# One decode step on one core: the last of wo's 32 row groups loaded on all 128 partitions, not on 64

## The chip, the core and the metric

The kernel runs on one core of a Trainium2 chip. The metric is device time in microseconds of one launch. The median of three runs of the kernel before is 100.18 us; the runs lie between 100.13 and 102.2 us. The profiled execution took 100.13 us, of which its page covers a span of 98.7 us, from the first instruction to the last.

## What is computed

One token `x` (1 x 1024, bf16) goes through an attention layer and an MLP that stand side by side, and the results are added.

```python
def reference(x, k_cache, v_cache, wq, wo, w1, b1, w2, b2):
    xn = layernorm(x)
    # attention: 32 query heads, 4 key/value heads of 128, the last 4096 positions
    q = xn @ wq                               # wq 1024 x 4096
    p = softmax(q k^T / sqrt(128));  o = p v  # per head
    attn = o.reshape(4096) @ wo               # wo 4096 x 1024
    # MLP on the layernorm of xn
    h = gelu(layernorm(xn) @ w1 + b1)         # w1 1024 x 3584
    mlp = h @ w2 + b2                         # w2 3584 x 1024
    return x + attn + mlp
```

With one token every weight is used once, so the kernel is a stream of loads with small products behind it: wq 8 MB, keys 4 MB, w1 7 MB, values 4 MB, w2 7 MB, wo 8 MB (counted as 1024 x 1024 bytes). The matmuls have the token's numbers as the stationary operand (128 x 1) and 512 columns of the weight as the moving one.

## The kernel before

All large loads are issued by the SyncE queue, in the order in which they are used: the first part of wq, the keys, the rest of wq, w1 in two halves, the values. w2 goes into the buffer of w1, and wo into the buffer of wq, so these loads wait until the second half of the w1 product is done (`pe_h`). The part that the change touches begins there.

`wo_pm` lays the 4096 rows of wo out so that partition p holds rows 32p to 32p+31; below, "row group r" is row 32p+r for every p, 2 KB on each of 128 partitions, 256 KB in all. Groups 0 to 30 are loaded into `WA` in seven pieces of 12, 9, 4, 2, 2, 1 and 1 groups. Group 31 is loaded apart, in eight small loads into the old key buffer `KT`: it is laid on partitions 0 to 63 alone, two rows (`s`) beside each other on each partition, and each small load covers eight partitions that lie four apart.

```python
WO_CHUNKS = [12, 9, 4, 2, 2, 1, 1]
...
wo_pm = A_wo.rearrange("(p j) n -> p (j n)", j=32)
wo_e = A_wo.rearrange("(s q e c j) n -> j q c e s n", s=2, q=2, e=8, c=4, j=32)
...
sp.wait_ge(PE.sem, pe_h)
c0 = 0
for j, nch in enumerate(W2_CHUNKS):                       # w2: 14 and 14
    sp.dma_start(W2[:, ...], w2_pm[:, ...]).then_inc(s_w2[j], 16)
    ...
j0 = 0
for j, nj in enumerate(WO_CHUNKS):
    sp.dma_start(WA[:, j0 * D:(j0 + nj) * D], wo_pm[:, j0 * D:(j0 + nj) * D]).then_inc(s_wo[j], 16)
    j0 += nj
    if j == 0:
        for q in range(2):
            for c in range(4):
                p0 = 32 * q + c
                sp.dma_start(KT[p0:p0 + 29:4, 0:2 * D].rearrange("e (s n) -> e s n", s=2),
                             wo_e[31, q, c]).then_inc(s_we, 16)
```

The attention output is put on 128 partitions as `OP`, one column for each row group. Because group 31 lies on 64 partitions, the upper half of the last column is copied down to partitions 0 to 63 as well (`OPX`).

```python
dve.wait_ge(PE.sem, pe_op)
DVE.mark(dve.tensor_copy(OP[:, :], PS[:, 512: 512 + 32]))
d_op = DVE.mark(dve.tensor_copy(OPX[:, :], PS[64:128, 512 + 31: 512 + 32]))
pe.wait_ge(DVE.sem, d_GT)
for j in range(len(W2_CHUNKS)):
    w2_rows(j)                                            # 56 matmuls into ACC[0], ACC[1]
```

The product with wo comes last. TensorE waits for each piece of wo, and multiplies two halves of 512 columns for each row group into the same accumulators as w2. After the first piece it does group 31 in four matmuls of 64 partitions. The output row is then copied out of PSUM, half by VectorE and half by ScalarE, and stored.

```python
pe.wait_ge(DVE.sem, d_op)
r = 0
for j, nj in enumerate(WO_CHUNKS):
    pe.wait_ge(s_wo[j], 16)
    for _ in range(nj):
        for n in range(2):
            last = pe.matmul(ACC[n], lhsT=OP[:, r:r + 1], rhs=WA[:, ...],
                             start=False, stop=(r == 30))
        r += 1
    if j == 0:
        pe.wait_ge(s_we, 8 * 16)
        for lhsT, c in ((OP[0:64, 31:32], 0), (OPX[:, :], D)):
            for n in range(2):
                pe.matmul(ACC[n], lhsT=lhsT, rhs=KT[0:64, c + n * 512: c + (n + 1) * 512],
                          start=False, stop=False)
pe_fin = PE.mark(last)
dve.wait_ge(PE.sem, pe_fin)
d_out = DVE.mark(dve.tensor_copy(OUT[32:33, :], ACC[1]))
act.wait_ge(PE.sem, pe_fin)
a_out = ACT.mark(act.activation(out=OUT[0:1, :], in_=ACC[0], func=ACTF.Copy))
```

Of the kernel before, what the change touches and what calls it, by code (L numbers as in the profile page):

```python
# [4 lines left out]
dt = mybir.dt  # L5
# [4 lines left out]
D = 1024  # L10
# [11 lines left out]
WQ_CHUNKS = [1, 3, 4]  # L22
W1_CHUNKS = [4, 4]
W2_CHUNKS = [14, 14]
WO_CHUNKS = [12, 9, 4, 2, 2, 1, 1]


class Track:
# [11 lines left out]
def bass_parallel_sum__sliding_block_cached__mixer_channel_mlp__decode_kernel(  # L40
# [20 lines left out]
    pe, dve, act, pool, sp = nc.tensor, nc.vector, nc.scalar, nc.gpsimd, nc.sync  # L61
# [7 lines left out]
    s_v = [nc.alloc_semaphore(f"s_v{g}") for g in range(HKV)]  # L69
    s_w2 = [nc.alloc_semaphore(f"s_w2{j}") for j in range(len(W2_CHUNKS))]  # L70
    s_wo = [nc.alloc_semaphore(f"s_wo{j}") for j in range(len(WO_CHUNKS))]
    s_we = nc.alloc_semaphore("s_we")
    s_out = [nc.alloc_semaphore(f"s_out{n}") for n in range(2)]

    PE = Track(nc, "S_PE")
    DVE = Track(nc, "S_DVE")
# [3 lines left out]
    def sb(name, shape, dtype):  # L80
        return nc.alloc_sbuf_tensor(name, shape, dtype)
# [37 lines left out]
    OHF = sb("OHF", [32, DH], dt.float32)  # L119
    OH = sb("OH", [32, DH], dt.bfloat16)  # L120
    OP = sb("OP", [128, 32], dt.bfloat16)
    OPX = sb("OPX", [64, 1], dt.bfloat16)
    OUT = sb("OUT", [33, 512], dt.bfloat16)
    KV = sb("KV", [128, HKV * W + HKV * NBLK * DH], dt.bfloat16)
    KT = KV[:, 0:HKV * W]
# [4 lines left out]
    PS = nc.alloc_psum_tensor("PS", [128, 8 * 512], dt.float32)  # L130

    ACC = [PS[32 * n: 32 * n + 1, (6 + n) * 512: (7 + n) * 512] for n in range(2)]
# [5 lines left out]
    w1_pm = B_w1.rearrange("(p k) n -> p (k n)", k=KC)  # L138
    w2_pm = B_w2.rearrange("(p c) n -> p (c n)", c=FC)
    wo_pm = A_wo.rearrange("(p j) n -> p (j n)", j=32)  # L140
    wo_e = A_wo.rearrange("(s q e c j) n -> j q c e s n", s=2, q=2, e=8, c=4, j=32)
    out_row = out.rearrange("b s n -> (b s) n")


# [14 lines left out]
    r = 0  # L159
# [136 lines left out]
    for j, nr in enumerate(WQ_CHUNKS):  # L296
        pe.wait_ge(s_wq[j], 16)
        for _ in range(nr):
            for n in range(2):
                for t in range(4):  # L300
                    c = k * NQ + t * 1024 + n * 512
                    last = pe.matmul(  # L302
                        PS[32 * t: 32 * t + 1, n * 512:(n + 1) * 512],
                        lhsT=XNTb[:, k:k + 1], rhs=WA[:, c: c + 512],
                        start=(k == 0), stop=(k == KC - 1))
# [19 lines left out]
    for i in range(4):  # L325
        p0, p1 = 32 * i, 32 * (i + 1)
# [11 lines left out]
    for g in range(HKV):  # L338
        for j in range(4):
            u = g * 4 + j  # L340
            for n in range(2):
                rhs = KT[:, g * W + n * 2048: g * W + (n + 1) * 2048].rearrange(
                    "p (b j a) -> p b j a", j=4, a=32)[:, :, j, :]
                last = pe.matmul(  # L344
                    PS[:, (4 + n) * 512:(5 + n) * 512],
                    lhsT=LQ[:, u * 128:(u + 1) * 128], rhs=rhs,
                    start=(u == 0), stop=(u == 15))
# [6 lines left out]
    for n in range(2):  # L354
        for t in range(4):
            pe.matmul(PS[32 * t: 32 * t + 1, (2 + n) * 512:(2 + n) * 512 + HW],  # L356
                      lhsT=identb[0:8, 2 * t + n: 2 * t + n + 1], rhs=B1R[:, :],
                      start=True, stop=False)
# [54 lines left out]
    j0 = 0  # L413
    for j, nj in enumerate(WO_CHUNKS):
        sp.dma_start(WA[:, j0 * D:(j0 + nj) * D], wo_pm[:, j0 * D:(j0 + nj) * D]).then_inc(s_wo[j], 16)  # L415
        j0 += nj
        if j == 0:

            for q in range(2):
                for c in range(4):  # L420
                    p0 = 32 * q + c
                    sp.dma_start(KT[p0:p0 + 29:4, 0:2 * D].rearrange("e (s n) -> e s n", s=2),  # L422
                                 wo_e[31, q, c]).then_inc(s_we, 16)


    dve.wait_ge(PE.sem, pe_h)
# [26 lines left out]
    for r in range(4):  # L453
        n = r // 2
        pe.matmul(ACC[n][:, (r % 2) * 256:(r % 2 + 1) * 256],
                  lhsT=identb[:, 32 * r: 32 * r + 1], rhs=XR[:, :],
                  start=False, stop=False)
# [16 lines left out]
    for b in range(NBLK):  # L474
        last = pe.matmul(PS[0:32, 0:512].rearrange("p (g d) -> p g d", g=HKV),  # L475
                         lhsT=PT[:, b * 32:(b + 1) * 32], rhs=Vb[:, b, :, :],
                         start=(b == 0), stop=(b == NBLK - 1))
# [25 lines left out]
    for q in range(4):  # L503
        last = pe.matmul(PS[:, 512: 512 + 32],
                         lhsT=SEL[:, q * 128:(q + 1) * 128], rhs=OH[:, q * 32:(q + 1) * 32],
                         start=(q == 0), stop=(q == 3))
    pe_op = PE.mark(last)
    dve.wait_ge(PE.sem, pe_op)
    DVE.mark(dve.tensor_copy(OP[:, :], PS[:, 512: 512 + 32]))
    d_op = DVE.mark(dve.tensor_copy(OPX[:, :], PS[64:128, 512 + 31: 512 + 32]))  # L510
    pe.wait_ge(DVE.sem, d_GT)
    for j in range(len(W2_CHUNKS)):
        w2_rows(j)
# [3 lines left out]
# [5 lines that stand above are left out]
                last = pe.matmul(  # L522
                    ACC[n], lhsT=OP[:, r:r + 1],
                    rhs=WA[:, r * D + n * 512: r * D + (n + 1) * 512],
                    start=False, stop=(r == 30))
            r += 1
        if j == 0:
            pe.wait_ge(s_we, 8 * 16)
            for lhsT, c in ((OP[0:64, 31:32], 0), (OPX[:, :], D)):
                for n in range(2):  # L530
                    pe.matmul(ACC[n], lhsT=lhsT, rhs=KT[0:64, c + n * 512: c + (n + 1) * 512],
                              start=False, stop=False)
    pe_fin = PE.mark(last)

    dve.wait_ge(PE.sem, pe_fin)
# [39 lines left out]
```

## Time and profile before

| | |
|---|---|
| median of three runs | 100.18 us |
| span of the profile | 98.7 us |
| TensorE busy with matmuls | 51.5 us (52% of the span), 342 matmuls |
| VectorE busy | 35.8 us (36%) |
| ScalarE, GpSimd busy | 5.8 us, 4.6 us |
| moved by DMA | 39.89 MB, mean 404 GB/s over the span |
| mean granted TensorE clock | 0.844 |

On the page, "L415" is line 415 of the kernel, "SPq" is the queue of SyncE that issues the loads, and PE is TensorE. A row such as `PE PS L522` stands for matmuls at line 522 that write the PSUM tensor `PS`. "DMA WA<-in_A_wo_dram" in the chain means that the next step waited for a load of wo into `WA`. The row of digits called "DMA" gives, for each of 40 equal slices, the mean busy share of the core's 16 DMA engines in tenths. Beside the page, the trace holds one record for each packet of a DMA engine (start, duration, bytes, queue), and one for each increment by which a load reports to its semaphore: a load over 128 partitions leaves 16 of these, which come one by one as the DMA engines finish their shares. The prediction calls them the completion records.

### The profile page before, as it was taken

To read this page: it belongs to the slowest core of one execution; us is meant where nothing else is said; L and a number is where in the kernel's file an instruction comes from. 1 tells how busy PE (TensorE), PEld (TensorE's weight loads), DVE (VectorE), ACT (ScalarE), POOL (GpSimd) and SP (SyncE) were. 2 spreads that over 40 slices of the span, in tenths; PEclk is the share of its full clock that TensorE was granted. 3 is DMA by queue.
4 is the path that set the end of the run, shared out by engine and by line. 5 is a ranking of instruction groups with operands and counts; after the bars stand their busy time and mean duration, and the time that the engine had idled before them with its cause. 6 is when DMAs were issued, how large, how long until landed. Compare 5 with 4: busy or idle time off the path is not lost.

```text
span 98.7 us, 834 instructions
## 1 busy us (share of the span) xinstructions
PE 51.5 (52%) x342; PEld 17.8 (18%) x342; DVE 35.8 (36%) x54; ACT 5.8 (6%) x11; POOL 4.6 (5%) x15
## 2 busy tenths in 40 slices
PE   0002600009100945999974006999469950799961
PEld 0002200002000302344331002334123310222210
DVE  4338599999991053000449700000440000000002
ACT  0500150000000002000040000000000000000002
POOL 6830000000000000000000000000000000000000
PEclk9999999999975588599999855559975998557999
DMA  5999999989999989999999999999998999999950
GB/s 153 425 426 425 425 455 458 468 382 438 425 425 467 465 384 407 500 390 407 389 422 422 428 525 398 395 500 395 402 465 384 468 428 393 411 421 398 404 198 1
DMA packets 3394, 39.89 MB, mean 404 GB/s; under 512 B 432, under 2 KB 448, under 8 KB 1088
## 3 DMA queue, kind: packets, MB, share of 16 engines
q1 hardware_dynamic: 3362, 39.85, 95.6%
q8 instruction: 2, 0.03, 0.1%
q10 hardware_dynamic: 30, 0.01, 0.0%
HBM read 39.86 MB, written 0.00 MB: 404 GB/s over the span
## 4 chain that ended last, share of the span: by engine, by line
DMA 53%; SPq 23%; PE 18%; DVE 3%; issue 1%
DMA WA<-in_A_wq_dram 29%; DMA WA<-in_A_wo_dram 24%; SPq L415 14%; PE PS L344 9%; SPq L422 6%; PE PS L302 4%; PE PS L368 3%; SPq L153 2%; DVE TT L311 1%; SPq L411 1%; DVE OUT L536 1%; DVE LQ L331 1%; SPq L149 1%; PE PS L356 0%; PE PS L522 0%
## 5 line engine op out<-in xcount | busy, mean ns | idle before, releaser
L291 DVE STREAM_TRANSPOSE KV<-KV 128x4096 bf16<-128x4096 bf16 x4 | 17.4, 4413 | 0.0
L302 PE MATMUL PS<-WA,XNTb 128*1 128x512 bf16 x64 | 7.3, 621 | 17.2 <-DMA WA<-in_A_wq_dram 17.2
L475 PE MATMUL PS<-KV,PT 128*32 128x512 bf16 x32 | 10.0, 489 | 6.2 <-DMA KV<-in_A_v_cache_dram 6.2
L522 PE MATMUL PS<-WA,OP 128*1 128x512 bf16 x62 | 10.3, 474 | 5.4 <-DMA WA<-in_A_wo_dram 5.4
L536 DVE CAST OUT<-PS 1x512 bf16<-1x512 f32 x1 | 0.7, 683 | 23.8 <-PE PS L522 23.8
L344 PE MATMUL PS<-KV,LQ 128*128 128x512 bf16 x32 | 8.8, 443 | 0.7 <-DVE LQ L331 0.7
L495 PE MATMUL PS<-W,GT 128*1 128x512 bf16 x56 | 7.9, 452 | 0.0
L475 PEld LDWEIGHTS PS<-KV,PT 128*32 128x32 bf16 x32 | 3.7, 118 | 12.0 <-issue 10.1
L302 PEld LDWEIGHTS PS<-WA,XNTb 128*1 128x1 bf16 x64 | 1.7, 109 | 22.0 <-DMA WA<-in_A_wq_dram 19.1
L480 DVE TENSOR_TENSOR OHM<-PS,RM 32x512 f32<-32x512 f32 x1 | 0.7, 680 | 13.3 <-PE PS L475 13.3
L522 PEld LDWEIGHTS PS<-WA,OP 128*1 128x1 bf16 x62 | 2.8, 96 | 12.8 <-issue 7.6
L256 PE MATMUL PS<-XT,onesf 128*128 128x16 f32 x2 | 0.6, 383 | 7.6 <-DVE XT L252 7.6
L344 PEld LDWEIGHTS PS<-KV,LQ 128*128 128x128 bf16 x32 | 3.5, 111 | 5.6 <-issue 2.3
L377 DVE TENSOR_REDUCE MXP<-PS 128x1 f32<-128x1024 f32 x1 | 1.2, 1224 | 8.9 <-PE PS L344 8.9
L495 PEld LDWEIGHTS PS<-W,GT 128*1 128x1 bf16 x56 | 2.7, 96 | 4.8 <-issue 2.3
L368 PE MATMUL PS<-W,YTb 128*1 128x448 bf16 x64 | 3.4, 352 | 0.0
L311 DVE STREAM_TRANSPOSE TT<-PS 128x1024 f32<-128x1024 f32 x1 | 1.2, 1250 | 5.6 <-PE PS L302 5.6
L538 ACT ACTIVATE OUT<-PS 1x512 bf16<-1x512 f32 x1 | 0.6, 586 | 40.9 <-PE PS L522 40.9
L398 ACT ACTIVATE Pe<-PS,NMB 128x512 bf16<-128x512 f32 x2 | 1.3, 683 | 12.4 <-DVE NMB L395 12.4
L333 ACT ACTIVATE LQ<-PS 32x128 bf16<-32x128 f32 x2 | 0.5, 268 | 24.0 <-PE PS L318 23.9
L186 DVE MEMSET PS<- 128x2048 f32 x1 | 1.8, 1765 | 0.4 <-issue 0.4
L218 POOL MEMSET LQ<- 128x2176 bf16 x1 | 1.9, 1902 | 0.0
(87 smaller groups left out, 27.5 us busy)
## 6 DMA issues: line engine op xcount, KB each, us to landing
W<-in_B_w_dram SPq DMA_DIRECT2D x4, 3584.0 KB, 30.6
KV<-in_A_k_cache_dram SPq DMA_DIRECT2D x4, 1024.0 KB, 9.8
WA<-in_A_wq_dram SPq DMA_DIRECT2D x1, 4096.0 KB, 28.5
KV<-in_A_v_cache_dram SPq DMA_DIRECT2D x4, 1024.0 KB, 50.4
WA<-in_A_wq_dram SPq DMA_DIRECT2D x1, 3072.0 KB, 19.4
WA<-in_A_wo_dram SPq DMA_DIRECT2D x1, 3072.0 KB, 31.6
WA<-in_A_wo_dram SPq DMA_DIRECT2D x1, 2304.0 KB, 30.7
WA<-in_A_wq_dram SPq DMA_DIRECT2D x1, 1024.0 KB, 5.1
```

What stands on the lines that cost most here:

```text
L153: sp.dma_start(KT[:, g * W:(g + 1) * W], A_k_cache[0, g, SK - W:SK, :].rearrange("(m b) d -> m (b d)", m=128),).then_inc(s_k[g], 16)
L218: c_lq = POOL.mark(pool.memset(LQ[:, :], 0.0))
L291: d_k.append(DVE.mark(dve.transpose(out=KT[:, g * W:(g + 1) * W], in_=KT[:, g * W:(g + 1) * W])))
L302: last = pe.matmul(PS[32 * t: 32 * t + 1, n * 512:(n + 1) * 512], lhsT=XNTb[:, k:k + 1], rhs=WA[:, c: c + 512], start=(k == 0), stop=(k == ...
L311: DVE.mark(dve.transpose(out=TT[:, :], in_=PS[:, 0:1024]))
L344: last = pe.matmul(PS[:, (4 + n) * 512:(5 + n) * 512], lhsT=LQ[:, u * 128:(u + 1) * 128], rhs=rhs, start=(u == 0), stop=(u == 15))
L368: last = pe.matmul(PS[32 * t: 32 * t + 1, (2 + n) * 512:(2 + n) * 512 + HW], lhsT=YTb[:, k:k + 1], rhs=W1[:, c: c + HW], start=False, stop ...
L415: sp.dma_start(WA[:, j0 * D:(j0 + nj) * D], wo_pm[:, j0 * D:(j0 + nj) * D]).then_inc(s_wo[j], 16)
L422: sp.dma_start(KT[p0:p0 + 29:4, 0:2 * D].rearrange("e (s n) -> e s n", s=2), wo_e[31, q, c]).then_inc(s_we, 16)
L475: last = pe.matmul(PS[0:32, 0:512].rearrange("p (g d) -> p g d", g=HKV), lhsT=PT[:, b * 32:(b + 1) * 32], rhs=Vb[:, b, :, :], start=(b == ...
L495: pe.matmul(ACC[n], lhsT=GT[:, c:c + 1], rhs=W2[:, c * D + n * 512: c * D + (n + 1) * 512], start=False, stop=False)
L522: last = pe.matmul(ACC[n], lhsT=OP[:, r:r + 1], rhs=WA[:, r * D + n * 512: r * D + (n + 1) * 512], start=False, stop=(r == 30))
```

## The change

Row group 31 is loaded like the others: it becomes part of the first piece of wo, which grows from 12 to 13 row groups, on all 128 partitions. The eight small loads, the semaphore they report to, the copy `OPX` and the four matmuls on 64 partitions are gone, and two matmuls on 128 partitions are added for the 32nd row group. It is meant to keep every row group in one layout and to give the 16 DMA engines equal shares of it. The order of scores and the first half of h, which the title of the change also names, is the same in both kernels.

```diff
-WO_CHUNKS = [12, 9, 4, 2, 2, 1, 1]
+WO_CHUNKS = [13, 9, 4, 2, 2, 1, 1]
...
-    s_we = nc.alloc_semaphore("s_we")
...
-    OPX = sb("OPX", [64, 1], dt.bfloat16)
...
-    wo_e = A_wo.rearrange("(s q e c j) n -> j q c e s n", s=2, q=2, e=8, c=4, j=32)
...
         sp.dma_start(WA[:, j0 * D:(j0 + nj) * D], wo_pm[:, j0 * D:(j0 + nj) * D]).then_inc(s_wo[j], 16)
         j0 += nj
-        if j == 0:
-
-            for q in range(2):
-                for c in range(4):
-                    p0 = 32 * q + c
-                    sp.dma_start(KT[p0:p0 + 29:4, 0:2 * D].rearrange("e (s n) -> e s n", s=2),
-                                 wo_e[31, q, c]).then_inc(s_we, 16)
...
-    DVE.mark(dve.tensor_copy(OP[:, :], PS[:, 512: 512 + 32]))
-    d_op = DVE.mark(dve.tensor_copy(OPX[:, :], PS[64:128, 512 + 31: 512 + 32]))
+    d_op = DVE.mark(dve.tensor_copy(OP[:, :], PS[:, 512: 512 + 32]))
...
-                    start=False, stop=(r == 30))
+                    start=False, stop=(r == 31))
             r += 1
-        if j == 0:
-            pe.wait_ge(s_we, 8 * 16)
-            for lhsT, c in ((OP[0:64, 31:32], 0), (OPX[:, :], D)):
-                for n in range(2):
-                    pe.matmul(ACC[n], lhsT=lhsT, rhs=KT[0:64, c + n * 512: c + (n + 1) * 512],
-                              start=False, stop=False)
```

## The prediction

> **What bounds the kernel now.** I read the chain of waits first, from its end:
>
> ```profile
> 72.63 23.65 DMA WA<-in_A_wo_dram
> 96.28 0.04 issue
> 96.33 0.40 PE PS L522 x2
> 96.73 0.02 issue
> 96.75 0.68 DVE OUT L536
> ```
>
> The columns are start, length and what was waited for. The last load of wo lands at 96.28 us; behind it stand two matmuls, the copy of the output and its store, a fixed tail of about 2.4 us up to 98.7. So the end is the landing of the last piece plus a constant. The waits say the same of TensorE, and the page of the load stream:
>
> ```profile
> PE PS L522 <- DMA WA<-in_A_wo_dram: 5.4, 4, 4.2
> ```
>
> ```profile
> DMA  5999999989999989999999999999998999999950
> ...
> q1 hardware_dynamic: 3362, 39.85, 95.6%
> q8 instruction: 2, 0.03, 0.1%
> ```
>
> The 16 DMA engines are busy almost from the first slice to the last but one, so the question is what the change does to the work of the engine that finishes last. The "q8" line is the one to notice: two packets of instructions went over the same engines, though not in the load queue. The last 6 us of the DMA view (window 91 to 97) show that the engines do not finish together:
>
> ```profile
> DMA  9798999999999999999987676676452000000000
> GB/s 464 328 492 328 355 382 382 437 410 437 423 410 396 369 437 382 396 410 396 382 328 287 232 287 246 246 273 259 191 191 96 27 0 0 0 0 0 0 0 0
> ```
>
> A slice is 0.15 us. The rate falls from about 400 to about 250 GB/s at some 94.2 us and stays there for over a microsecond. A group of engines is idle by then while others work. The completion records name the groups. For three pieces of wo, the 16 times in order (us):
>
> ```
> groups 0-11  : 82.50 82.63 82.63 82.70 82.72 82.75 82.80 82.81 82.81 82.85 82.89 82.93 83.04 83.27 | 84.35 84.46
> groups 12-20 : 88.12 88.13 88.20 88.30 88.34 88.77 | 89.36 89.59 89.61 89.64 89.67 89.72 89.77 89.85 | 89.87 89.97
> group 30     : 94.52 94.52 94.59 94.69 94.74 95.11 | 95.69 95.89 95.93 95.94 95.97 96.03 96.08 96.13 | 96.16 96.28
> ```
>
> Before the small loads of group 31 there are 14 engines together and two **late** ones, 1.1 to 2.0 us behind. After them there are six early engines and ten late ones. Eight of the ten must be those that the small loads went to: the 8 loads left 72 completion records, 8 of them at 54.59 to 59.61, one soon after each issue, and 64 at 82.71 to 84.68, which is 8 engines for each load. The other two are the two that were late already. They cannot be among the eight, or they would be late twice, near 91.4 instead of 89.97. So the load of group 31 sits on eight engines that don't hold the two late ones, and it makes them just as late.
>
> Where do the two come from? The record of w1's first half (39.74 to 40.50) has no straggler; its second half has one (15 by 49.01, the last at 50.08); w2's first half still one (67.46, then 68.54); its second half two (75.95, then 77.05 and 77.16). The two instruction packets are at 42.77 us (16384 bytes, 1.069 us) and 69.83 us (16384 bytes, 1.061 us). Each falls between a record without and a record with one more straggler, and its length is the gap. In the DMA view of window 42 to 44 and of window 69 to 71 there is one such packet each:
>
> ```profile
> q1 hardware_dynamic: 30, 0.86, 101.6%
> q8 instruction: 1, 0.02, 3.3%
> ```
>
> [...] in a stream that is full, the packet pushes back one engine's later loads by 1.07 us, and nothing gives that back.
>
> **The change part by part.**
>
> *Removed: the eight small loads.* On each of the eight engines they are 8 x 2 packets of 2 KB. The trace has these 128 packets at a mean of 84 ns, so 16 x 0.084 = 1.34 us, and eight completion writes of 9 ns, 0.07 us: 1.4 us. The records agree: the medians of the early six and of the middle eight of groups 12-20 are 88.25 and 89.66.
>
> *Added: 2 KB on each of 128 partitions in the first piece.* That is 8 packets on each of 16 engines that grow from 24 to 26 KB. The mean packet of 24576 bytes takes 914 ns, that of 28672 bytes 1069 ns, so 2048 bytes more cost 155 / 2 = 78 ns, and eight of them 0.62 us. As a check, one more row group on its own moves the last record from 95.66 (group 29) to 96.28 (group 30), 0.62 us.
>
> *Sum at the last piece of wo, by group of engines:*
>
> | engines | last record now | change | then |
> |---|---|---|---|
> | the eight with small loads | 96.13 | -1.4 + 0.62 | 95.35 |
> | the six early | 95.11 | +0.62 | 95.7 |
> | the two behind an instruction packet | 96.28 | +0.62 | 96.9 |
>
> Total work falls a little (8 x 0.78 saved against 8 x 0.62 added), but only the last row counts: **+0.62 us**. I don't take off anything for the two engines having the memory to themselves at the end: 2 KB packets that start after 95.4 us, when few run, still take 84 ns.
>
> *SyncE.* The eight issues take 5.83 us of its queue (53.36 to 59.19), and wo's other pieces will be issued that much sooner. That is worth nothing: the last three issues already stall (4.48, 7.41 and 7.26 us) with loads queued ahead of them, and the last is issued at 79.89, some 15 us before its data come.
>
> *TensorE.* Four matmuls of 64 partitions go and two of 128 come. The first piece starts at 84.60 and gets 24 matmuls done by 89.8 at a granted clock of about half (0.53 in 84.5 to 90.4), 0.43 us a pair; group 31 follows until 90.43. Afterwards the start is near 85.2, and 13 pairs take 5.6 us, until 90.8. The second piece lands at 89.97 + 0.62 = 90.6, so there is 0.2 us of backlog, which goes by at the full clock that holds from 90.4 (1.00 in the table by stretches): nine pairs in 1.9 us, and the next piece lands at 93.1. The last pieces wait for data, as now.
>
> *VectorE.* The copy `OPX` (0.16 us at 72.83) lies 11 us ahead of its use. Nothing.
>
> Sum: 98.7 + 0.6 = 99.3 us of span, 100.18 + 0.62 = **100.8 us**.
>
> **The rivals.** (1) *The bytes are spread evenly, so the end comes sooner.* Over sixteen equal engines, removing 1.4 us from eight and adding 0.62 to all would bring the end 0.8 us forward, to 99.4. For it speaks that the middle eight end only 0.15 us before the last. Against it: the two late engines get the added bytes and none of the relief. It holds only if the stragglers change engine, or if the instruction packets fall elsewhere. Both packets come ahead of the first changed TensorE instruction, so I see no cause for that. (2) *TensorE becomes the end.* If the clock stayed at half for the rest, 32 pairs from 85.2 would last 13.7 us, to 98.9, about 2 us later than the data: near 102.8. The clock was at full from 90.4 and the load on TensorE hardly changes, so this is only a tail; it is why the range reaches further upward. (3) *Hidden anyway.* If the last piece of wo had slack, the time would not move. The chain shows none: 0.04 us between the landing and the matmul.
>
> **The range and the chances.** The step is 0.62 us if the late engines are the same two. Packet lengths could make it 0.4 to 0.9. The runs before spread upward (100.13, 100.18, 102.2), so I take 100.3 to 101.5. Two per cent are 2.0 us: slower by over that needs rival 2 (0.02), faster by over that nothing here would give (0.01).
>
> **What would show it.** The "KV<-in_A_wo_dram" issues are gone and the first piece of wo is 3328 KB. The last landing in the chain is near 96.9 instead of 96.28, the tail after it the same. The two instruction packets are again near 42.8 and 69.8. The completion records of the last piece fall into 14 together by about 95.7, and two near 96.8 and 96.9. If all 16 come together at about 95.5, the stragglers were not what I took them for; if the chain ends in a run of matmuls without a wait for data, it is rival 2.

## The result: 0.4 us slower, as the late engines would have it

The changed kernel takes 100.59 us (median of five runs, 100.44 to 100.9) against 100.18 us, a ratio of 1.0044 (95% interval 1.0022 to 1.0065). That is slower by 0.2 to 0.65%, well inside 2%, and 0.2 us under the predicted 100.8. It holds against the lower of two groups of times that the kernel before turned out to have; over all runs taken side by side later, the means of the two kernels lie 0.07 us apart (last experiment below). The ratios here and below leave out runs more than 1.5% above the fastest of the same kernel; what is left of the kernel before can still mix its two groups.

The chain of waits of the changed kernel, from its end (start, length, what was waited for), has the same form as before and has moved as a whole:

```profile
56.88 39.83 DMA WA<-in_A_wo_dram
96.70 0.04 issue
96.75 0.40 PE PS L511 x2
97.15 0.02 issue
97.17 0.68 DVE OUT L519
```

The last piece of wo lands at 96.70 us instead of 96.28; the two matmuls, the copy and the gaps have the lengths of before. The load starts much earlier in this chain (issued at 56.88, not 72.63), as the small loads no longer stand in SyncE's queue, and lands later all the same.

The page shows the stream as full as before, and again two packets of instructions:

```profile
DMA  5999999989999989989799998998998989999930
...
q1 hardware_dynamic: 3170, 39.85, 95.1%
q8 instruction: 2, 0.03, 0.1%
```

The DMA view of the last 6 us (window 91 to 97, slices of 0.15 us) has changed its form:

```profile
DMA  9999899999999997999999997421111111100000
GB/s 410 437 437 410 328 492 382 437 382 437 410 410 437 382 437 301 382 396 396 396 382 396 396 369 273 150 82 55 55 41 55 55 41 55 41 0 0 0 0 0
```

Before, ten engines shared the last microsecond at about 250 GB/s. Now the full rate holds until 94.6 us, nearly all engines stop together, and for a further microsecond some 55 GB/s are left. The completion records show two engines behind it, so about 27 GB/s each. For the piece with groups 0-12 and for the last one:

```
groups 0-12 : 83.26 83.27 83.31 83.32 83.33 83.34 83.38 83.39 83.44 83.47 83.51 83.55 83.57 83.66 | 84.89 84.90
last piece  : 95.15 95.16 95.19 95.21 95.22 95.23 95.26 95.28 95.31 95.36 95.38 95.42 95.45 95.53 | 96.69 96.70
```

Fourteen engines are done by 95.53, two by 96.70. (The last piece now holds the 32nd group.) The instruction packets were at 42.78 and 75.98 us.

### The profile page after: what moved, and what is told of

It is laid out like the page before. It is cut to its first block, busy times and chain, and to the rows that moved or that the text cites. A ratio compares the mean times of both kernels' runs of the same rounds, so it can differ in the third digit from the quotient of the medians.

```text
span 99.1 us, 821 instructions
## 1 busy us (share of the span) xinstructions
PE 51.1 (52%) x340; PEld 17.7 (18%) x340; DVE 35.6 (36%) x53; ACT 5.8 (6%) x11; POOL 4.6 (5%) x15
## 4 chain that ended last, share of the span: by engine, by line
DMA 69%; PE 19%; SPq 6%; DVE 3%; issue 1%
DMA WA<-in_A_wo_dram 40%; DMA WA<-in_A_wq_dram 29%; PE PS L341 10%; PE PS L299 4%; PE PS L365 3%; SPq L412 3%; SPq L150 2%; DVE TT L308 1%; SPq L408 1%; DVE OUT L519 1%; DVE LQ L328 1%; SPq L146 0%; PE PS L353 0%; PE PS L511 0%; PE PS L389 0%
## 5 line engine op out<-in xcount | busy, mean ns | idle before, releaser
L511 PE MATMUL PS<-WA,OP 128*1 128x512 bf16 x64 | 9.7, 441 | 7.2 <-DMA WA<-in_A_wo_dram 7.1
L465 PE MATMUL PS<-KV,PT 128*32 128x512 bf16 x32 | 9.3, 462 | 4.9 <-DMA KV<-in_A_v_cache_dram 4.9
L341 PE MATMUL PS<-KV,LQ 128*128 128x512 bf16 x32 | 10.0, 489 | 0.7 <-DVE LQ L328 0.7
```

Of the source, the lines that this page charges most:

```text
L341: last = pe.matmul(PS[:, (4 + n) * 512:(5 + n) * 512], lhsT=LQ[:, u * 128:(u + 1) * 128], rhs=rhs, start=(u == 0), stop=(u == 15))
L511: last = pe.matmul(ACC[n], lhsT=OP[:, r:r + 1], rhs=WA[:, r * D + n * 512: r * D + (n + 1) * 512], start=False, stop=(r == 31))
```

## The experiments

The theory: two DMA engines are late because each carried one packet of TensorE's instructions, and the two alone set the end; so what counts is what those two are given. Main rival: the two engines are late for another reason.

### Taking the instruction packets away

```diff
 # in short: the changed kernel; 61 of 340 matmuls stay, all waits and loads as they were
-for u in ...: for n in range(2): matmul(scores)      +only u == 0
-for b in range(NBLK): matmul(p v)                    +only b == 0
-for c in w2 chunk / r in wo piece / k in w1 half     +only the first of each; q: row 0 and two matmuls
```

> The changed kernel with most matmuls left out (57 of 340 stay, so TensorE has about 115 matmul and weight-load instructions, fewer than the 170 it had begun when the first instruction packet came). All loads and their order stay; the output is not the reference's. Theory (two DMA engines are late because each carried one packet of TensorE's instructions): no instruction packet beside the loads, the 16 completion records of the last piece of wo within 0.5 us of each other, near 95.5 instead of 96.70, a span near 98.0 and a time near 99.4, about 1.1 us less than the changed kernel and 0.8 below the kernel before. Rival (the two engines are slower for a reason of their own, or for the load stream's sake): two records stay about 1.2 us behind and the last landing stays near 96.7.

It leaves out most of the arithmetic (61 matmuls stay, not the 57 of the forecast), so its time is that of the stream of loads with little behind it. Measured: 99.5 us (ratio to the kernel before 0.9885, 0.9805 to 0.9966), 1.1 us under the changed kernel. The queues on its page hold no instruction packet any more:

```profile
q1 hardware_dynamic: 3170, 39.85, 96.0%
q10 hardware_dynamic: 30, 0.01, 0.0%
```

Its DMA view of window 91 to 97 has no tail, and its chain starts the end at 95.45:

```profile
DMA  9999989999999999999999995200000000000000
```

```profile
54.09 41.36 DMA WA<-in_A_wo_dram
95.45 0.04 issue
```

All 16 records of the last piece lie between 95.07 and 95.45. The same loads in the same order, without the packets: no late engine. The rival that the engines are slow in themselves, or for the sake of the loads, falls. That it is the packets, and not the matmuls that went with them, rests on the next experiment as well.

### One packet more

```diff
+        for _ in range((80, 48, 0)[j]):     # while TensorE waits for wq
+            pe.matmul(PS[64:65, 3328:3336], lhsT=XNTb[:, 0:1], rhs=XNTb[:, 0:8], start=True, stop=True)
```

> The changed kernel with 128 tiny matmuls more (256 TensorE instructions), in the two gaps in which TensorE waits for wq. Their result is not used. Theory: one more packet of 16384 bytes of instructions, so three records of the last piece of wo behind the others, or one of them twice as far (about 2.2 us); in the first case the end moves by less than 0.3 us, in the second it is near 97.8, a time near 101.7. Rival (engines slow in themselves): two late records as in the changed kernel, whatever TensorE fetches.

The page and the chain:

```profile
q8 instruction: 3, 0.05, 0.2%
```

```profile
56.66 39.98 DMA WA<-in_A_wo_dram
96.64 0.04 issue
```

The third packet is at 16.6 us, and the records of the last piece end 95.41 | 96.51 96.60 96.64: three late engines in place of two, each late once. The time is 100.55 us (median of 20 runs), that of the changed kernel. So each packet of 16384 bytes makes one engine late (the 256 added instructions brought one), and the end here doesn't care how many are late, only how late the last is.

How late is more than the gap of 1.1 us to the record before, which belongs to the slowest of the other engines. Against the median of the others the three are 1.3 to 1.5 us behind, and the two of the changed kernel 1.4. The packet records of these two profiles show two parts: an instruction packet takes 0.98 to 1.11 us, and within 0.02 us of its end there starts a load packet that takes 1.46 to 1.57 us, 0.5 us more than the mean of its size (in the changed kernel 1.57 us against 1.07 for 28 KB, and 1.46 against 0.99 for 26 KB). The packet and this extra time together are about 1.5 us. (The records don't name the engine; that it is the same one is inferred from the times.)

### The old layout without the packets

The kernel before, with the same matmuls left out (65 of 342 stay, not 59).

> The kernel before with the same matmuls left out as in the changed kernel with few matmuls (59 stay; the output is not the reference's), loads and their order unchanged. Theory: no instruction packet, so the last landing is that of the eight engines with the small loads, near 96.1, against 95.45 in the changed kernel without packets: with the late engines gone, spreading group 31 evenly is now the better choice by about 0.65 us, and this kernel is at 100.0 to 100.2 us, no faster than with its packets. For the spread of the kernel before (a group near 100.1 to 100.5, a group near 101.4 to 101.9): if that comes from instruction packets on engines that also carry the small loads, this kernel has one group only, within 0.4 us. Rival (the spread comes from the small loads alone): a second group about 1.3 us higher stays.

Measured: 100.25 us (ratio 0.9988, 0.9968 to 1.0008). The tail of ten engines has become one of eight; DMA view of window 91 to 97, and the end of the chain:

```profile
DMA  6979989999999999999975545555532000000000
```

```profile
96.22 0.04 issue
96.26 0.61 PE PS L523 x2
```

The records of the last piece are eight at 94.53 to 94.78 and eight at 95.87 to 96.22. Against 95.45 with even shares, the small loads on eight engines now cost 0.77 us at the last landing (0.65 was expected), and the times of the two kernels without packets, 100.25 and 99.5 us, differ by 0.75. **This is the whole change in one table**, last landing of wo in one profile each:

| | with instruction packets | without |
|---|---|---|
| small loads on eight engines (before) | 96.28 | 96.22 |
| even shares (changed) | 96.70 | 95.45 |

The small loads on eight engines cost nothing only if late engines stand among the other eight, since the eight then finish just ahead of them. Even shares win 0.8 us in the stream without late engines, and lose 0.4 in the one with two.

### Which engines are late

```diff
+for m in range(1, 16):      # behind the last piece of wo: 64 bytes on each of m partitions
+    sp.dma_start(KT[0:m, ...32 elements...], wo_pm[0:m, 0:32]).then_inc(s_pr[m - 1], 16)
```

No record names its engine, so engines are numbered here by probe, from 0: engine 11 is the one that a probe of 12 partitions adds to those of a probe of 11. A first form had probes of 2 KB on 9 to 15 partitions behind the first piece of wo:

> The changed kernel with seven probe loads behind the first piece of wo, of 9, 10, 11, 12, 13, 14 and 15 partitions, 2 KB each, into the old key buffer; nothing reads them. [...] Theory (the two late engines are fixed ones outside the first eight): the loads of few partitions show no late record, and from some number on one and then two records are late by about 1.2 us; the numbers at which they appear name the two engines. Rival (the late engines are among the first eight and the small loads of the kernel before went elsewhere): both late already in the load of 9. The end is some 0.5 us later than in the changed kernel at most, 96.8 to 97.2.

The probe of 11 partitions has no late record (the last at 85.33), that of 12 has one (86.61, the others by 85.52), that of 13 two (86.60 and 86.79). So engines 11 and 12 are late. That each partition of a probe has an engine of its own, and that a larger probe uses the engines of the smaller ones and one more, was the author's assumption; one late record from 12 partitions on and two from 13 fit it. But the run took 102.42 us with the last landing at 98.61, over a microsecond later than expected: probes of this size disturb what they look at. So the probes were made tiny and put behind everything, in both kernels.

> The kernel before with fifteen tiny probe loads (64 bytes on each of 1, 2, ... 15 partitions[...]) behind the last piece of wo. A late engine shows in every probe from its number on, so the probes name the two engines behind the instruction packets. New theory, from the spread of the kernel before in the runs so far (a group near 100.1, a group near 101.3): the instruction packets do not keep to fixed engines, but go to neighbouring engines, others in each execution. If both named engines are among numbers 8 to 15: last landing of wo near 96.3, time near 100.2. If one is among 0 to 7, which also carry the small loads of group 31: last landing 97.3 to 97.7, time near 101.3. Rival (the packets always go to the same engines, 11 and 12 as in the probed run so far): those two again, and near 100.2.

> The changed kernel with the same fifteen probes behind the last piece of wo. New theory: two neighbouring late engines, whichever they are, last landing 96.5 to 96.9 and a time of 100.4 to 100.9, the same for all engine numbers, as all engines have equal shares. Rival (fixed engines): 11 and 12.

> The kernel before with the fifteen probes once more. New theory: other engine numbers than in the first run of it; with both among 8 to 15 the time is near 100.2 and the last landing near 96.3, with one among 0 to 7 near 101.3 and 97.3 to 97.7. Rival (fixed engines): the same numbers and the same time as in the first run.

The fifteen probes, of 120 partitions in all, bring 240 packets of under 512 bytes to the kernel before (672 in the first of these runs against 432), which fits one of data and one that reports for each partition. The data records of four probes of the first of these runs. The small loads of group 31 keep engines 0 to 7 busy up to 96 us and later: the probes of eight or fewer partitions have no data record before 96 us, the one of nine has its first at 94.94.

```
11 partitions: 95.03 95.09 95.27             | 96.84 96.98 97.08 97.23 97.50 97.58 97.84 98.30
12 partitions: 95.20 95.26 95.44 96.30       | 97.05 97.17 97.28 97.42 97.67 97.75 98.01 98.48
13 partitions: 95.38 95.43 95.63 96.34 96.48 | 97.26 97.38 97.48 97.61 97.86 97.93 98.19 98.66
14 partitions: 94.98 95.56 95.61 95.80 96.52 96.67 | 97.47 ...
```

Engines 8 to 10 are early (95.03 to 95.27 in the probe of 11 partitions), 11 and 12 are late (96.34 and 96.48 in that of 13), 13 is early again: the probe of 14 has four early records and two late ones. The second run of it says the same (with 12 partitions a record at 96.73 is new, with 13 one at 96.27), and so does the changed kernel (new records at 96.98 and 96.79, then at 95.46 with 14). The times are 101.01 and 100.52 us for the kernel before and 100.63 us for the changed one, with the wait for the probes at the end of each; the last landings of wo are 96.31, 96.56 and 96.80. So in every profiled execution that was probed the late engines are 11 and 12, outside the first eight. The theory that they change from one execution to the next found no support here; it falls for these executions.

### Even shares, but in eight small loads

```diff
-WO_CHUNKS = [13, 9, 4, 2, 2, 1, 1]
+WO_CHUNKS = [12, 9, 4, 2, 2, 1, 1]
+for i in range(8):          # behind the first piece
+    sp.dma_start(WA[16*i:16*(i+1), 31*D:32*D], wo_pm[16*i:16*(i+1), 31*D:32*D]).then_inc(s_we, 16)
...                         # TensorE waits for s_we and does group 31 behind the first piece
```

> Group 31 apart as in the kernel before, in eight small loads behind a first piece of 12 groups, but each of 16 partitions into its place on all 128 partitions: as many small loads and as much time of SyncE's queue as before, with every engine getting 16 KB as in the changed kernel. Theory (only which engines get the bytes matters): the last landing near that of the changed kernel, 96.7 to 96.9, two records behind 14; time 100.5 to 100.8. Rival (the small loads or their issue are what makes the kernel before faster): as the kernel before, 100.2, last landing 96.3.

A miss. The last landing is at 97.96, the time 101.76 us (1.0111, 1.0052 to 1.017). (The eight issues took 3.7 us of SyncE's queue, not the 5.8 of the kernel before; the longest stall behind them is 7.4 us in both. The page has 496 packets of under 512 bytes against 368 of the changed kernel, so 16 reports for each small load; the kernel before has 432, so eight.) So it is not the number of small loads that helped the kernel before. But equal shares alone don't make it the changed kernel either: the 128 packets of 2 KB took a mean of 117 ns (84 in the kernel before), and the 128 packets of 18 KB of the next piece up to 1285 ns, with a mean of 776 against 692. Together that is 128 x 33 ns + 128 x 84 ns = 15 us of engine time, 0.9 us on each of 16, most of the 1.1 to 1.3 us by which the last landing is later than in the changed kernel (96.70 and 96.83). A guess was that engines hinder each other when they write to neighbouring partitions, so the same loads were laid eight partitions apart.

> The eight small loads of 16 partitions again, each on partitions eight apart instead of 16 neighbours. Theory (16 engines that write to neighbouring partitions hinder each other): the packets of 2 KB take a mean of 84 to 100 ns instead of 117, the last landing comes down from 97.96 to 96.7 to 97.4, and the time to between 100.6 and 101.2. Rival (eight small loads on 16 engines cost this much wherever they are laid): 97.8 to 98.0, time near 101.8.

The guess falls: a mean of 122 ns, last landing at 98.26, 101.84 us (1.0101, 1.0071 to 1.0132). The chains of the two runs:

```profile
66.64 31.32 DMA WA<-in_A_wo_dram
97.96 0.04 issue
```

```profile
66.82 31.44 DMA WA<-in_A_wo_dram
98.26 0.04 issue
```

What does slow them stays open. The small loads of the kernel before lie four partitions apart, go to eight engines and write to `KT` (84 ns a packet); these go to 16 engines and write to `WA`, on neighbouring partitions (117 ns) or eight apart (122 ns). Spacing, engines and buffer changed together, and no run here parts them.

### The kernels again, and the spread of the kernel before

> The changed kernel itself, beside many runs of the kernel before. New theory: its runs lie close together, 100.4 to 100.9, between the two groups of the kernel before (near 100.1 and near 101.3), so that the means of both kernels differ by less than 0.3 us when both groups of the kernel before turn up. Theory of the prediction as it stands (the late engines never carry the small loads): all runs of the kernel before near 100.2, the changed kernel 0.4 to 0.6 us slower.

> The kernel before as it is, a look for an execution of its slower group. If its time is over 101: records of the last piece of wo with one or two engines 2.2 to 2.8 us behind the first (small loads and an instruction packet on the same engine), last landing near 97.5. If the slower group has another cause: 14 engines and two as in the known execution, and the time lost elsewhere. If it is near 100.2: last landing near 96.3 again.

> The same kernel again, with the same two readings: near 100.2 with the last landing near 96.3, or over 101 with one or two engines 2.2 to 2.8 us behind the first.

The changed kernel: 100.65 us over 22 runs (100.47 to 100.94), ratio 1.0031 (1.0012 to 1.005), last landing 96.83. The kernel before, profiled twice more: 100.18 us both times, last landings 96.21 and 96.33. Neither was an execution of the higher group, so that group was never seen in a profile.

There is such a group: of 97 runs of the kernel before beside these experiments, 57 lie between 99.79 and 100.53 us and 40 between 101.01 and 101.95. The changed kernel shows none of it in its 22 runs here, and the kernel before without instruction packets has 21 of 22 runs between 100.05 and 100.49, the other at 102.65. Counting all runs beside it, the changed kernel has a mean of 100.67 and the kernel before one of 100.60 (27 runs). So the forecast of two groups with equal means came true, and the theory that all runs of the kernel before lie near 100.2 did not.

An instruction packet on an engine that also carries the small loads would make such a group, and only in that kernel. Its size fits: an engine that ends near 96.1 and is put back by 1.5 us would end near 97.6, an estimated 1.3 us after 96.28, and the medians of the groups (100.2 and 101.42) are 1.2 us apart. But it is argued from the two absences, and not shown: no profile of that kernel has an engine that late. The experiment without packets also takes away most of TensorE's work. The granted clock does not tell the groups apart: it lies between 0.844 and 0.931 in the lower and between 0.846 and 0.932 in the higher.

## Why the prediction was right

**The end is a landing plus a constant.** Right: 2.42 us from the last landing to the end of the span before (96.28 to 98.7), 2.4 after (96.70 to 99.1).

**Two engines are late by an instruction packet each.** Right, and shown by taking the packets away and adding one. Two details were not. The cost of a packet is not its own length of 1.07 us: that is the gap to the slowest other engine, and in groups 0-11 of the kernel before the two late records are 1.5 and 1.7 us behind the median of the other fourteen. The sum was not touched by this, as it starts from the late records as they stand. And the second packet, foreseen near 69.8 us, came at 75.98. Its time is no sign of anything, since five profiles of the kernel before (two of them with probes) have it at 69.76, 69.83, 74.91, 75.98 and 76.82, always before the first piece of wo has landed.

**The change relieves the wrong engines.** Right. The prediction's table gave 95.35 for the eight, 95.7 for the six and 96.9 for the two; the records have fourteen at 95.15 to 95.53 and two at 96.69 and 96.70. That the late engines lie outside the eight is shown for the probed executions, by the probes; for the higher group of times it is open.

**The size, 0.62 us.** It came out at 0.42 in this pair of profiles; over the three unprobed profiles of the kernel before (96.28, 96.21, 96.33) and two of the changed one (96.70, 96.83) the difference of the means is 0.49. The term of the eight longer packets was right: a late engine's way through the first piece of wo is 84.90 - 76.99 = 7.91 us with 13 groups and 84.46 - 77.16 = 7.30 with 12, 0.61 more. What the sum left out is where the late engine stands when that piece begins. The last record of w2 came in at 76.99 instead of 77.16 in this pair, though no load had been changed up to there (77.10 and 77.20 in the other two unprobed profiles of the kernel before, 77.12 in the other one of the changed kernel). That is the scatter from one execution to the next, and the range had room for it at its lower end, though for another reason (packet lengths).

**The spread of the kernel before.** The prediction took the one run at 102.2 us for upward spread. Of the 97 later runs 40 lie at 101.01 us or more, and against those the changed kernel is the faster one. So there is some luck in the match: four of the five runs with which it was compared fell into the lower group. With 57 of 97 runs in that group, a median of five falls into it about two times in three (an estimate).

**SyncE's issues are worth nothing.** Right. The issues of wo come without the long stalls now; from the view by tile (min, median and max in ns, first and last start):

```profile
L412 SPq DMA_DIRECT2D WA<-in_A_wo_dram x7: 431/432/2151, 54.0 to 56.9; - x7
```

The longest takes 2.2 us instead of 7.4, and the last one starts 16 us sooner. The end came no sooner for it.

**TensorE has no part in it.** Right, with its step off to the safe side. From the timeline of TensorE:

```profile
85.03 4.66 PE L511 MATMUL PS<-WA,OP 128*1 128x512 bf16 x26 [4.81 <-DMA WA<-in_A_wo_dram]
90.43 2.11 PE L511 MATMUL PS<-WA,OP 128*1 128x512 bf16 x18 [0.74 <-DMA WA<-in_A_wo_dram]
```

The granted clock was 0.71 in 84.5 to 90.4, not 0.53, so 13 pairs took 4.66 us rather than 5.6. TensorE then waited 0.74 us for the second piece where 0.2 us of backlog were foreseen. Rival 2 never came near.

**Rival 1**, the gain of 0.8 us from even shares, is what a stream without late engines gives: 96.22 against 95.45, 0.77.

## What to carry to other kernels

When the stream of loads is the bound, ask for the work of the engine that ends last, not for the sum: read the completion records of one load, in order, before and after each suspect. A layout that looks uneven can be the even one once the late engines are counted, and its merit goes when the cause of the lateness goes. The instruction stream can have a price in such a kernel even where its engine is not the bound: here each instruction packet of 16384 bytes put one DMA engine back by about 1.5 us, and the time was 100.59 us with two of them (340 matmuls) and 99.5 with none (61).

## What was not expected of the hardware

The late engines, numbered by probe, were 11 and 12 in all four probed executions (the first late record with 12 partitions, the second with 13), and not others from one to the next. Behind each instruction packet of about 1 us, one load packet took 0.5 us longer than its like (1.57 us against a mean of 1.07 and 1.46 against 0.99 in the changed kernel). Small loads of 2 KB a partition on 16 engines took a mean of 117 and 122 ns a packet in the two layouts tried, where those on eight engines took 84, and the large packets beside them were slower (up to 1285 and 1300 ns for 18 KB, against a mean of 692 in the kernel before). Eight fewer small loads in SyncE's queue took away nearly all of its long stalls (7.4 us before, 2.2 after), with the same bytes queued ahead; the two layouts with eight small loads of 16 partitions have a stall of 7.4 us again.
